# One wait more for a POOL memset, and one filler more, in a decode attention and MLP kernel

## The chip, the cores and the metric

The kernel runs on one core of a Trainium2 chip. The metric is the device time in microseconds (us) of one execution, as the median of several runs. The core has five engines with a queue of instructions each: PE (TensorE, matrix products), DVE (VectorE), ACT (ScalarE), POOL (GpSimd) and SP (which here only issues DMAs). They wait for each other by semaphores.

## The reference

A decode step of one token for 8 sequences: attention over the last 2048 positions of a cache, a small MLP beside it, and a gate that mixes both.

```python
# x: 8 x 1 x 576; caches: 8 x 16 heads x 8192 x 128, bf16; 32 query heads, W = 2048
q = (x @ wq) as 32 heads of 128
k, v = the last W rows of k_cache, v_cache, each head used by two query heads
p = softmax(q k^T * 128**-0.5);  a = (p v) @ wo          # wo: 4096 x 576
y = layernorm(x);  b = gelu(y @ w1 + b1) @ w2 + b2       # w1: 576 x 4608, w2: 4608 x 576
g = sigmoid(sum(x * gate_w));  out = g * a + (1 - g) * b
```

The two caches' windows make up 134 of the 154 MB that are read.

## The kernel before, in words

The keys and values are cut into 16 items each: item n = 4g + i holds 32 of the 128 (sequence, head) pairs (group g) and a quarter i of their window, 4 MB in bf16. Items are loaded in the order K0, K1, V0, K2, V1, ..., K15, V14, V15, each into the next of four slots of the `arena` in SBUF, and then the bias `b2`, the first 24 of 36 column blocks of w2 (two DMAs of 1728 KB), wo (four DMAs of 1152 KB) and the rest of w2 (1152, 432 and 144 KB). All these DMAs are issued by SP in that order (L624, L847, L859, L829); a DMA that reuses a slot makes SP wait until the work that read the slot is done.

For a key item, VectorE transposes four parts (`tr`, L691) and TensorE multiplies each with the queries into four PSUM banks (`qk`, L709 and the helper line L175). VectorE takes the maximum over the banks (`mx`, L642, 128x2048 from PSUM) and updates the running one (`nb`, L646, 128x1), ScalarE takes the exponentials (L648), and VectorE transposes them (`pt`, L666) into `PT`. The result is spread onto the diagonal blocks of a zeroed P tile by four copies, one for each quarter of the partitions (`qrx`, L740 on ScalarE, L741 on POOL or VectorE). Against that tile TensorE multiplies the value item: 64 products, some written out and the others in a loop (`pv`, L753 and the helper line L186). In this text, block n is the 64 products of value item n. VectorE adds the block to the running output (`o`, L796).

For the first 14 items two quarters of the copies go to POOL and two to ScalarE; for items 14 and 15 one goes to ScalarE and three to VectorE (`px_engs`).

The P tile of items 0 to 14 lies at a fixed place, zeroed once by a memset on POOL (`ptx0`, L604); the copies always write the same diagonal blocks. The P tile of item 15, the last, has a home of its own, in the room of the transposed keys (`KT`), which is free once the last `qk` is done. It is zeroed by a second memset on POOL, `o_kz` (`ktx0`, L724, 128x4096 fp32), whose only dependency is that last `qk` (it is added at the end of `k_unit`). The copies of item 15 wait for it (`px_free`). A line near the change orders the maximum of item 15 behind VectorE's three copies of item 14 in VectorE's queue, without a semaphore.

The order in each queue comes from a planner (`_Plan.schedule`), which takes the ready operation with the earliest start by modelled costs; entries in `deps` become semaphore waits, entries in `after` only order.

`keep_warm` issues fillers on TensorE: products of a zero tile with a mask, into a PSUM bank that is not in use. There are ten behind the last `qk` (before block 14), six between blocks 14 and 15, and three (`warm1`) behind the projection with the fourth wo block.

After block 15 come: the sum over the pairs of a group (`vmul`, `acc` on VectorE, `ew` on POOL L804, `us` on TensorE L807), with products of `b2` and w2 beside it on TensorE (`m2_b`, `m2_0`); the output's scaling and transposition (L810, L811); then on TensorE the second 24 products of w2, the four projections with wo (16 products each), `warm1`, and the last 24 products of w2 in three parts (16, 6 and 2), each of which waits for its own DMA. These products have line L580. At last two copies out of PSUM and two small DMAs of the output.

Of the kernel before, what the change touches and what calls it, by code (L numbers as in the profile page):

```python
# [38 lines left out]
class _Plan:  # L39
# [10 lines left out]
    def add(self, eng, fn, deps=(), name=None, cost=0.1, after=(), prio=0):  # L50
        op = _Op(eng, fn, deps, name, cost, after=after, prio=prio)
        op.idx = len(self.all)
        self.all.append(op)
        return op

    def dma(self, eng, fn, semkey, nbytes, deps=(), name=None, after=(), prio=0):
        op = _Op(eng, fn, deps, name, self.DMA_ISSUE, after=after, is_dma=True, dma_sem=semkey, nbytes=nbytes, prio=prio)
        op.idx = len(self.all)
        self.all.append(op)
        return op  # L60
# [113 lines left out]
def held_matmul(nc, e, out, lhsT, rhs, start=False, stop=True, skip=False, tile_size=(128, 128), tile_position=(0, 0)):  # L174
    return e.add_instruction(mybir.InstMatmult(  # L175
        name=nc.get_next_instruction_name(), engine=mybir.EngineType.PE,
        ins=[e.lower_ap(rhs), e.lower_ap(lhsT)], outs=[e.lower_ap(out)],
        start_tensor_calc=start, stop_tensor_calc=stop, is_transpose=False, bass_skip_group_check=skip,
        tile_size=tile_size, tile_position=tile_position, ldweights=False))
# [13 lines left out]
def build_kernel(nc, A_x, A_k_cache, A_v_cache, A_wq, A_wo, B_x, B_w1, B_b1, B_w2, B_b2, gate_w, out):  # L193
# [28 lines left out]
    with ExitStack() as es:  # L222
# [83 lines left out]
        def view(name, parts=128):  # L306
            o, n, dt = R[name]
            a = arena[0:parts, o // 2: o // 2 + (n * (2 if dt == BF else 4)) // 2]
            if dt == F32:
                a = a.bitcast(F32)  # L310
            return a
# [47 lines left out]
        def slot(s):  # L359
            return RAW[:, s * DE:(s + 1) * DE]  # L360
# [247 lines left out]
        pt_done, px_done, pv_done = {}, {-1: [o_px0]}, {}  # L608
# [6 lines left out]
        def take_slot():  # L615
            n = n_slot[0]
            n_slot[0] += 1
            return (1, 2, 0, 3)[n % ND]
# [105 lines left out]
        o_kz = add("pool", lambda e: e.memset(view("KT").bitcast(F32), 0.0), deps=[], name="ktx0", cost=4.5, prio=3)  # L724

        def v_item(n):
# [16 lines left out]

            if n == NL - 2:
                mx_done[n + 1].after.extend(op for op in px_done[n] if op.eng == "dve")

            def pv_part(a, b):
                def fn(e):
                    mm = None
                    for k in range(a, b):  # L750
                        lhsT = bass.AP(arena, offset=px_at + 128 * k, ap=[[AST, 128], [1, 128]])
                        rhs = bass.AP(arena, offset=aoffs("RAW") + s * DE + 128 * k, ap=[[AST, 128], [SE, 2], [1, 128]])
                        mm = e.matmul(ps[:, ob_, 0:256], lhsT, rhs, start=(k == 0), stop=True, skip_group_check=True)  # L753
                    return mm
                return fn
# [60 lines left out]
        def keep_warm(name, n, after, banks=(0, 1, 2, 3), deps=None):  # L816
            def fn(e):
                mm = None
                for k in range(n):
                    args = (ps[:, banks[k % len(banks)], :], zeros_bf, maskR)  # L820
                    mm = e.matmul(*args, start=True, stop=True, skip_group_check=True) if k == 0 else held_matmul(nc, e, *args, start=True, stop=True, skip=True)
                return mm
            return add("pe", fn, deps=[o_z, o_mR] + (deps or [ex_done[NL - 1]]), name=name, cost=0.22 * n, after=after)

        def wo_all(_):
            def place(s, at, i):
                dst = slot(s)[:, at:at + WO_CH * D]
                h0 = WO_CH * i
                d = dma("sp", lambda e: e.dma_start(dst, A_wo[128 * h0:128 * (h0 + WO_CH), :].rearrange("(p j) c -> p (j c)", j=WOR)),  # L829
                        "o%d" % i, WO_CH * 128 * D * 2, deps=slot_free[s] if at == 0 else [], name="d_wo%d" % i, after=last_dma[-1:])  # L830
                last_dma.append(d)
                dj = dst.rearrange("p (j c) -> p j c", j=WOR)
                return AccGroup("proj%d" % i, [(oT[:, j, i, :], dj[:, j, :]) for j in range(WOR)], o_T + [d], cost=1.0, prio=1).op
            s = take_slot()
            done = [place(s, WO_CH * D * i, i) for i in range(3)]
            slot_free[s] = done
            s = take_slot()
            done = [place(s, 0, 3)]
            o_m2.append(keep_warm("warm1", 3, done))
            m2_at.append((s, WO_CH * D))  # L840
            slot_free[s] = done

        m2_at = []
        o_m2 = []
# [36 lines left out]
        for kind, i in stream:  # L881
            {"K": k_item, "V": v_item, "W": wo_all, "M": m2_chunk, "B": bias}[kind](i)
# [64 lines left out]
```

## Time and profile before

| | |
|---|---|
| median of 3 runs | 367.36 us (365.57 to 367.49) |
| the profiled execution | 366.66 us |
| its span | 365.4 us |
| mean granted clock of TensorE | 0.939 |
| busy: PE, DVE, ACT, POOL | 276.6, 256.7, 131.6, 76.1 us |
| data moved | 154.45 MB, 423 GB/s over the span |

All durations and times of day in this document are from the span's start of one profiled execution. The profile names an instruction by engine, line of the kernel, operation, what it writes and reads, and its shape; behind it, in brackets, the idle time of the engine before it and what ended that. Engines that are off the chain of waits may be idle at no cost. The granted clock is the share of TensorE's full speed that it was allowed to run at.

### The profile page before, as it was taken

How to read it: one execution, taken by the hardware profiler on the slowest of the kernel's cores; microseconds unless marked ns; L12 is line 12 of the kernel's file. 1: busy time of each engine (PE TensorE's matmuls, PEld its weight loads, DVE VectorE, ACT ScalarE, POOL GpSimd, SP SyncE). 2: the span in 40 equal slices, each digit the busy share in tenths (PEclk: the TensorE clock that was granted, in tenths of full speed). 3: DMA queues.
4: the chain of work that ended last, by engine and by line, in shares of the span. 5: the costliest groups of instructions: out<-in, count | busy, mean ns of one | idle time of the engine just before them, and what ended most of it. 6: DMA issues, size and time to landing. Idle time of an engine off the chain costs nothing.

```text
span 365.4 us, 4420 instructions
## 1 busy us (share of the span) xinstructions
PE 276.6 (76%) x1829; PEld 126.8 (35%) x1382; DVE 256.7 (70%) x196; ACT 131.6 (36%) x117; POOL 76.1 (21%) x76
## 2 busy tenths in 40 slices
PE   0455555999897958996969669786869697986997
PEld 0110000436171705370525225342516061602774
DVE  0722978797877696949395978767576969499511
ACT  1012106374444442644343325444444444402400
POOL 9123002130414040404121130304040404003000
PEclk9976596999998998999899999999999899999899
DMA  8999999999999999999999999999999999999993
GB/s 347 431 434 407 452 416 446 434 427 448 413 456 407 452 413 452 418 445 434 425 445 416 448 416 445 420 447 416 448 438 423 441 420 442 422 441 416 422 431 155
DMA packets 6578, 154.45 MB, mean 423 GB/s; under 512 B 764, under 2 KB 932, under 8 KB 1320
## 3 DMA queue, kind: packets, MB, share of 16 engines
q1 hardware_dynamic: 6512, 154.29, 98.2%
q8 instruction: 6, 0.10, 0.1%
q10 hardware_dynamic: 56, 0.03, 0.0%
q14 instruction: 4, 0.03, 0.0%
HBM read 154.31 MB, written 0.01 MB: 422 GB/s over the span
## 4 chain that ended last, share of the span: by engine, by line
DMA 45%; DVE 35%; PE 13%; issue 4%; ACT 2%; POOL 0%; ACTq 0%
DMA arena<-in_A_k_cache_dram 43%; DVE arena L691 20%; DVE arena L666 5%; PE ps L175 4%; PE ps L186 4%; DMA arena<-in_gate_w_dram 2%; PE ps L580 2%; DVE arena L642 2%; DVE arena L799 1%; DVE arena L741 1%; PE ps L502 1%; DVE arena L796 1%; PE ps L753 1%; PE ps L709 1%; DVE arena L563 1%
## 5 line engine op out<-in xcount | busy, mean ns | idle before, releaser
L691 DVE STREAM_TRANSPOSE arena<-arena 128x2048 f32<-128x2048 f32 x64 | 144.9, 2287 | 29.9 <-DMA arena<-in_A_k_cache_dram 28.3
L175 PE MATMUL ps<-arena 128*128 128x512 bf16 (+2 forms) x457 | 127.4, 427 | 11.7 <-DVE arena L691 8.7
L186 PE MATMUL ps<-arena 128*128 x942 | 107.1, 275 | 0.0
L186 PEld LDWEIGHTS ps<-arena 128*128 x942 | 92.8, 99 | 11.9 <-issue 0.3
L741 POOL COPY arena<-arena 32x2048 bf16<-32x2048 bf16 x28 | 52.8, 1885 | 206.7 <-DVE arena L666 205.9
L709 PE MATMUL ps<-arena 128*128 128x512 bf16 x120 | 49.3, 411 | 52.6 <-DVE arena L691 45.9
L740 ACT ACTIVATE arena<-arena 32x2048 bf16<-32x2048 bf16 x30 | 57.2, 1906 | 71.9 <-DVE arena L666 71.6
L648 ACT ACTIVATE arena<-ps,arena 128x2048 bf16<-128x2048 f32 x16 | 31.5, 1968 | 108.4 <-DVE arena L646 75.5
L709 PEld LDWEIGHTS ps<-arena 128*128 128x128 bf16 x128 | 13.1, 102 | 163.7 <-DVE arena L691 107.4
L642 DVE TENSOR_REDUCE arena<-ps 128x1 f32<-128x2048 f32 x16 | 36.7, 2291 | 31.8 <-PE ps L175 31.7
L666 DVE STREAM_TRANSPOSE arena<-arena 128x2048 bf16<-128x2048 bf16 x16 | 36.4, 2274 | 2.1 <-ACT arena L648 2.1
L652 ACT ACTIVATE ps<-arena 128x2048 f32<-128x2048 f32 x15 | 28.1, 1872 | 0.1
L753 PE MATMUL ps<-arena 128*128 128x256 bf16 x82 | 14.3, 272 | 3.5 <-DVE arena L741 3.5
L753 PEld LDWEIGHTS ps<-arena 128*128 128x128 bf16 x82 | 8.0, 99 | 18.6 <-issue 16.1
L453 PE MATMUL ps<-arena 8*128 8x8 bf16 x8 | 0.6, 171 | 14.6 <-DVE arena L427 9.5
L558 DVE TENSOR_TENSOR arena<-arena 128x1152 f32<-128x1152 f32 x1 | 1.4, 1358 | 11.5 <-ACT arena L556 11.5
L580 PE MATMUL ps<-arena 128*8 128x288 bf16 (+1 forms) x140 | 9.2, 286 | 0.0
L635 POOL COPY arena<-arena 32x128 bf16<-32x128 bf16 x16 | 4.6, 287 | 15.3 <-ACT arena L537 7.7
L724 POOL MEMSET arena<- 128x4096 f32 x1 | 3.5, 3511 | 20.0 <-PE ps L175 20.0
L804 POOL TENSOR_TENSOR arena<-arena 128x256 f32<-128x256 f32 x4 | 2.5, 613 | 23.7 <-DVE arena L802 23.7
L580 PEld LDWEIGHTS ps<-arena 128*8 128x8 bf16 (+1 forms) x140 | 6.0, 86 | 3.4 <-issue 1.4
L741 DVE COPY arena<-arena 32x2048 bf16<-32x2048 bf16 x6 | 7.0, 1160 | 0.2
(104 smaller groups left out, 94.1 us busy)
## 6 DMA issues: line engine op xcount, KB each, us to landing
arena<-in_A_k_cache_dram SPq DMA_DIRECT2D x16, 4096.0 KB, 27.1
arena<-in_A_v_cache_dram SPq DMA_DIRECT2D x16, 4096.0 KB, 27.0
arena<-in_B_w_dram SPq DMA_DIRECT2D x1, 4608.0 KB, 23.2
arena<-in_A_wo_dram SPq DMA_DIRECT2D x4, 1152.0 KB, 22.5
arena<-in_A_wq_dram SPq DMA_DIRECT2D x1, 4096.0 KB, 12.8
arena<-in_B_w_dram SPq DMA_DIRECT2D x2, 1728.0 KB, 24.5
arena<-in_B_w_dram SPq DMA_DIRECT2D x1, 1152.0 KB, 15.3
arena<-in_B_w_dram SPq DMA_DIRECT2D x1, 576.0 KB, 24.2
```

Source lines behind the costliest of these rows:

```text
L175: return e.add_instruction(mybir.InstMatmult(name=nc.get_next_instruction_name(), engine=mybir.EngineType.PE, ins=[e.lower_ap(rhs), e.lowe ...
L186: return e.add_instruction(mybir.InstMatmult(name=nc.get_next_instruction_name(), engine=mybir.EngineType.PE, ins=[operand(r, r_ap), opera ...
L580: ins = e.matmul(ps[32 * j:32 * j + 8, BK_ACC, 0:JN], lhsT, rhs[:, JN * j:JN * j + JN], start=False, stop=True, skip_group_check=True, til ...
L642: mx = mx_done[n] = add("dve", lambda e: e.tensor_reduce(out=k(n, MX), in_=ps[:, 0:4, :].rearrange("p a n -> p (a n)"), axis=AXL.X, op=ALU ...
L648: ex = add("act", lambda e: e.activation(out=Pm, in_=ps[:, 0:4, :].rearrange("p a n -> p (a n)"), func=ACTF.Exp, bias=k(n, NB), scale=SCAL ...
L652: mask_done[n + 1] = add("act", lambda e: e.activation(out=ps[:, 0:4, :].rearrange("p a (n c) -> p (a n) c", c=32), in_=bass.AP(arena_f, o ...
L666: pt_done[n] = add("dve", lambda e: e.transpose(bass.AP(arena, offset=aoffs("PT") + 2048 * (n % 2), ap=[[AST, 128], [1, 2048]]), Pm), deps ...
L691: tr = add("dve", (lambda rh=rh, hh=hh, kb=kb: lambda e: e.transpose(bass.AP(arena_f, offset=foffs("KT") + kb * 2048, ap=[[AST // 2, 128], ...
L709: mm = e.matmul(*args, start=False, stop=True, skip_group_check=True) if rc == 0 else held_matmul(nc, e, *args, stop=True, skip=True)
L740: return e.activation(out=dst, in_=src, func=ACTF.Copy)
L741: return e.tensor_copy(dst, src)
L753: mm = e.matmul(ps[:, ob_, 0:256], lhsT, rhs, start=(k == 0), stop=True, skip_group_check=True)
```

## The change

Two lines. The memset of the last P tile's home gets VectorE's copies of item 14 (its three quarters of the last P tile but one) as further dependencies, so that POOL waits for a semaphore of VectorE before it. And `warm1`, behind the projection of the fourth wo block (the fourth output block), has four fillers where it had three.

```diff
@@ -743,6 +743,7 @@
 
             if n == NL - 2:
                 mx_done[n + 1].after.extend(op for op in px_done[n] if op.eng == "dve")
+                o_kz.deps.extend(op for op in px_done[n] if op.eng == "dve")
 
             def pv_part(a, b):
                 def fn(e):
@@ -836,7 +837,7 @@
             slot_free[s] = done
             s = take_slot()
             done = [place(s, 0, 3)]
-            o_m2.append(keep_warm("warm1", 3, done))
+            o_m2.append(keep_warm("warm1", 4, done))
             m2_at.append((s, WO_CH * D))
             slot_free[s] = done
```

The order of instructions in all five queues is otherwise the same in both kernels. In POOL's queue the memset stands last but one, with `ew` of the last group (L804) behind it.

## The prediction

> **What bounds the kernel now.** I read the page's slices first: DMA is at 9 tenths in every slice but the last, at 423 GB/s on average, so up to the last key block the kernel runs at the rate at which its data arrive. The chain of waits (window 315 to 366 us) then shows where the order of work takes over:
>
> ```profile
> 318.48 6.61 DVE arena L691 x3
> ...
> 327.73 2.23 DVE arena L666
> ...
> 329.99 3.53 DVE arena L741
> ...
> 333.55 0.69 DVE arena L741
> ...
> 334.27 0.70 DVE arena L741
> ...
> 335.10 0.38 PE ps L753 x2
> ...
> 335.50 8.39 PE ps L186 x60
> ```
>
> From 318.5 us, where the last key block lands, the end is set by VectorE and then TensorE. To be seen: three equal copies of VectorE (L741, its three quarters of P tile 14) take 3.53, 0.69 and 0.70 us, and value block 14 on TensorE waits for the third. The timeline of the same window says what lies beside the slow one, and what it costs later:
>
> ```profile
> 329.47 3.51 POOL L724 MEMSET arena<- 128x4096 f32 x1 [20.05 <-PE ps L175]
> ...
> 334.99 2.29 DVE L642 TENSOR_REDUCE arena<-ps 128x1 f32<-128x2048 f32 x1
> ...
> 341.94 2.12 DVE L741 COPY arena<-arena 32x2048 bf16<-32x2048 bf16 x3
> ...
> 361.79 1.64 PE L580 MATMUL ps<-arena 128*8 128x288 bf16 x24
> ```
>
> The memset ends at 332.98 and the slow copy at 333.52, that is 0.54 us later, about a copy's own length: it has stood still for as long as POOL wrote. The same three copies for P tile 15, with POOL idle, take 2.12 us. An earlier stretch (timeline, 30 to 38 us) repeats it with POOL's other memset, which ends at 36.17:
>
> ```profile
> 32.66 3.51 POOL L604 MEMSET arena<- 128x4096 f32 x1 [5.24 <-PE ps L175]
> 33.80 1.36 DVE L558 TENSOR_TENSOR arena<-arena 128x1152 f32<-128x1152 f32 x1 [11.47 <-ACT arena L556]
> 35.19 1.59 DVE L559 TENSOR_SCALAR arena<-arena 128x1152 f32<-128x1152 f32 x1
> 36.82 1.36 DVE L560 TENSOR_TENSOR arena<-arena 128x1152 f32<-128x1152 f32 x1
> ```
>
> L559 ends 0.61 us behind the memset, while the two-input L558 takes its 1.36 us with the memset running as L560 does without. Last, the stretches of 1 us with the granted clock, third number from the end:
>
> ```profile
> 336.00:337.00 1.00, 1.00 (x9) 0.76 (x8) 1.00 (x1) 0.00 (x0) 0.00 (x0) 0.71 0.81 343
> 337.00:338.00 1.00, 1.00 (x6) 0.71 (x5) 0.44 (x2) 0.49 (x1) 0.00 (x0) 0.50 1.04 444
> ...
> 339.00:340.00 1.00, 1.00 (x7) 0.72 (x6) 0.40 (x1) 0.97 (x4) 0.00 (x0) 0.58 0.97 415
> ```
>
> TensorE stood idle from 331.56 (end of its ten fillers) to 335.10; soon after, its clock is halved from 336.42 to 339.84. The 60 looped matmuls of block 14 take 8.39 us; the same loop for block 12, at full clock (274.08), takes 6.71.
>
> **The change, step by step.**
>
> *The copies.* Without the memset they run 329.99 to 332.14 (2.12 us by the row of P tile 15). Saved: 2.83 us.
>
> *VectorE behind them.* The maximum L642 moves from 334.99 to 332.16 and now has the memset beside it (POOL starts some 0.1 us after the third copy, 332.25 to 335.76). Neither it nor the small L646 behind it is shown beside a memset. L642 reads PSUM; L796, which reads PSUM and SBUF, took 0.44 us beside a POOL copy at 288.33 as it does elsewhere, so I charge nothing; the upper end is a reduction that stands still until 335.76 (rival C). L646 has two SBUF inputs: like L558 beside a memset it would cost nothing, but L799, also with two, took 1.58 us beside a POOL copy (288.81) and 0.48 alone (353.22). The bounds are 0 and 335.76 - 334.47 = 1.3 us. I take 0, as L558 had a memset beside it and not a copy. A gain is excluded, since both already ran undisturbed.
>
> The Trainium skill ("GPSIMD Engine Reference", section Key points) says that POOL and VectorE contend where VectorE is in a two-port mode or has two SBUF inputs. The slow copy agrees; L558, with two inputs, did not slow down. By that rule L646 takes the 1.3 us, and the time below stays the same.
>
> *P tile 15.* Everything up to its copies moves by 2.83: exponentials 334.7, transpose L666 336.8 to 339.1, copies 339.1 to 341.23. The memset must be done by 339.1; it is at 335.76, so its later start is covered by 3.3 us. Behind the new wait POOL's queue holds only L804, needed at 354: nothing.
>
> *Block 14 on TensorE.* The ten fillers still end at 331.56, the block starts at 332.27: idle 0.7 us instead of 3.5, so no half clock; it lasts the 7.0 us of block 12 and ends at 339.3 instead of 344.1. The six fillers then end near 340.6.
>
> *Block 15* waited for block 14 and its fillers; now it waits for the copies: 341.36 instead of 345.38. This is 4.0 us, more than the copies gave, as the half clock goes too. Its 7.29 us end at 348.65.
>
> *The closing stage.* Everything on engines up to the projection moves by 4.0: L807 at 350.9, the next 24 products of w2 at 351.5, projections from 353.1.
>
> *SP.* The wait that holds the fourth block of wo and the last three pieces of w2 is block 14's end, so these four DMAs are issued 4.8 us earlier. They stand behind three wo blocks in one queue, and DMA is at 0.95 to 1.02 from 344 to 359 us. I take nothing for it: they land when they landed before (DMA issues from 344 to 346 us; the last number is us from issue to landing):
>
> ```profile
> arena<-in_A_wo_dram SPq DMA_DIRECT2D x1, 1152.0 KB, 12.9
> arena<-in_B_w_dram SPq DMA_DIRECT2D x1, 1152.0 KB, 15.3
> arena<-in_B_w_dram SPq DMA_DIRECT2D x1, 432.0 KB, 15.9
> arena<-in_B_w_dram SPq DMA_DIRECT2D x1, 144.0 KB, 15.7
> ```
>
> Their issues were at 344.1, 344.51, 344.97 and 345.45, so they land at 357.0, 359.8, 360.9 and 361.15. So the fourth projection, which could start at 356.0, starts at 357.05 and ends at 358.05; four fillers, 0.21 each by the chain (1.08 for five), end at 358.9; then TensorE waits 0.9 us for w2's piece.
>
> *The fourth filler* costs 0.21 us if that wait is not there; in it, nothing.
>
> *The end.* From 359.85 the last 24 products take their 1.64 us and end at 361.5, with the other two pieces landed in time (if they hold up the last eight: 361.75). Before, they ended at 363.43. **Sum: 1.7 to 1.95 us, taken as 1.9.** The remaining 2 us to the span's end are unchanged. The profiled execution, 366.66 us (span 365.4 and 1.26 around it), becomes 364.75. It lies 0.70 below the median of 367.36 of the runs shown; the same step from that median gives **365.4 us**. About half of the 4.0 us won upstream is lost to the data.
>
> **Rivals.**
>
> A. *The data come earlier too.* Issuing 4.8 us sooner could fill the gaps at 359 to 361, where DMA is busy 0.59 and 0.23. For: that share. Against: the queue was 13 to 15 us deep, so those transfers did not wait for their issue. Wholly unblocked, the last products would start at 357.9 and end at 359.55: gain 3.9 us, 363.5; partly, 364.5.
>
> B. *The clock halves at another place.* TensorE now waits 0.7 us before block 15 (1.9 if L646 is held), 1.0 before the fourth projection and 0.9 before the last products. For: an idle 2.41 us was followed by half clock at 288.6. Against: the same 2.41 us before 269.1 was not, and 1.46 and 1.67 us were never. Half clock in block 15 after a held L646: start 342.5, 1.7 us more, end 351.5, last products from 360.8 to 362.4, gain 1.0, 366.4. In the last products: 1.64 more, gain 0.3, 367.1.
>
> The Trainium skill ("TensorE: Matmul & The Clock Gate", Part 1) says that the clock follows activity in windows of about 3.4 us that run freely. The 3.42 us of half clock agree; by it the two waits at the end would have to fill most of one window, which they do not.
>
> C. *Slower: the memset takes the maximum as its victim.* It stands across L642 instead of the copy. If that waits for 335.76 it ends at 338.05, 0.77 later than before, and the copies of P tile 15 end at 344.85. Block 14 ended at 339.3, its fillers at 340.6: TensorE is idle for 4.3 us, and block 15 loses 1.7 us per 3.4 us of half clock, one or two such stretches. It starts at 344.95, 0.43 earlier, ends 1.3 to 3.0 later, and with the fourth filler the end is 1.5 to 3.2 us later: 368.9 to 370.6. It turns into a loss once L642 is held by more than some 2.1 us (4.0 less 1.7 and 0.2); here it is 3.6. For: the long copy was held in just this way. Against: L796 and L691 ran undisturbed beside POOL's copies.
>
> D. *The memset was not at fault*, and 3.53 us belong to that copy: 367.4 to 367.6. The 0.69 and 0.70 behind it speak against it.
>
> **Numbers.** A measurement of this kernel can tell about 0.5%, here 1.84 us, from no change. The forecast has 0.66; its 1.9 lies just beyond that bound, and I put 0.44 above and 0.22 below. A 0.14, B 0.10, C 0.09 (0.01 of it at its lower end, inside the bound), D 0.01. Faster: 0.44 + 0.14 = 0.58. Same: 0.22 + 0.10 + 0.01 + 0.01 = 0.34. Slower: 0.08. The range reaches to 363.9 (most of A) and 366.9 (the forecast with the spread of 1.9 us among the runs shown, and the first B); left out are C and the rests of A, B and D.
>
> **What would show it.** Right: L724 starts near 332.25; three copies of 0.70; L642 of 2.29 and L646 of 0.16 beside the memset; loop of block 14 near 6.7 us at clock 1.00; block 15 from about 341.4; a wait for data of about 1 us before the fourth projection and again behind the fillers; last products from 359.85. Wrong: a long L642; a half clock behind 340; or landings of the last w2 pieces that move with their issue.

## The result and the profile after

The changed kernel takes 364.67 us (median of 5 runs, 364.53 to 364.98) against 366.40 us for five runs of the kernel before on the same occasion: a ratio of 0.9947, with a 95% interval of 0.9925 to 0.9970. By the medians that is 1.7 us or 0.47% faster, by the ratio, which is not that of the medians, 0.53%; the interval excludes no change, but reaches to both sides of the 0.5% that the prediction set as its bound. The profiled execution took 364.70 us, with a span of 363.4 us. Of all runs below, two lie far out and count in no ratio: 415.0 us (one of six of `after_cut`) and 561.8 us (one of the kernel before).

The timeline of the changed kernel, 327 to 336 us. Behind the change, lines from 746 on carry a number that is one higher than before.

```profile
329.96 2.12 DVE L741 COPY arena<-arena 32x2048 bf16<-32x2048 bf16 x3
332.11 2.29 DVE L642 TENSOR_REDUCE arena<-ps 128x1 f32<-128x2048 f32 x1
332.19 3.51 POOL L724 MEMSET arena<- 128x4096 f32 x1 [22.57 <-DVE arena L741]
332.23 0.38 PE L754 MATMUL ps<-arena 128*128 128x256 bf16 x2 [0.70 <-DVE arena L741]
...
334.44 0.16 DVE L646 SCALAR_TENSOR_TENSOR arena<-arena 128x1 f32<-128x1 f32 x1
```

The three copies take 2.12 us together, as those of P tile 15 do. The memset now runs beside the maximum L642 and the small L646, and neither is longer for it: 2.29 and 0.16 us, as before. Block 14 starts after 0.70 us of idle time.

The closing stage in the timeline, 338 to 363 us:

```profile
341.34 0.38 PE L754 MATMUL ps<-arena 128*128 128x256 bf16 x2 [0.34 <-DVE arena L741]
...
351.72 4.58 PE L580 MATMUL ps<-arena 128*8 128x288 bf16 x72
...
357.01 1.15 PE L580 MATMUL ps<-arena 128*8 128x288 bf16 x16 [0.71 <-DMA arena<-in_A_wo_dram]
358.31 0.81 PE L175 MATMUL ps<-arena 128*128 128x512 bf16 x3 [0.16 <-issue]
...
359.78 1.73 PE L580 MATMUL ps<-arena 128*8 128x288 bf16 x24 [0.66 <-DMA arena<-in_B_w_dram]
```

Two waits for data, which the kernel before did not have, stand in the brackets: 0.71 us before the fourth projection and 0.66 us before the last 24 products. The chain of waits (315 to 364 us) says the same of the end:

```profile
332.62 6.72 PE ps L186 x60
...
339.69 0.23 SPq L830
...
339.96 19.77 DMA arena<-in_B_w_dram
...
359.78 1.75 PE ps L580 x24
```

Behind block 14 it no longer goes over VectorE and block 15, but over a w2 piece that SP issued once block 14 was done. Its 19.77 us are nearly all time in the queue, as the landing times show (DMA issues from 339.5 to 342 us, at 339.6, 339.96, 340.43 and 340.9):

```profile
arena<-in_A_wo_dram SPq DMA_DIRECT2D x1, 1152.0 KB, 17.4
arena<-in_B_w_dram SPq DMA_DIRECT2D x1, 1152.0 KB, 19.8
arena<-in_B_w_dram SPq DMA_DIRECT2D x1, 432.0 KB, 20.4
arena<-in_B_w_dram SPq DMA_DIRECT2D x1, 144.0 KB, 20.2
```

Issued 4.5 us earlier, they land at 357.0, 359.8, 360.8 and 361.1: within 0.1 us of where they landed before.

### The profile page after: what moved, and what is told of

It reads as the page before. It is cut to its first block, busy times and chain, and to the rows that moved or that the text cites. A ratio compares the mean times of both kernels' runs of the same rounds, so it can differ in the third digit from the quotient of the medians.

```text
span 363.4 us, 4421 instructions
## 1 busy us (share of the span) xinstructions
PE 274.3 (75%) x1830; PEld 125.7 (35%) x1382; DVE 253.9 (70%) x196; ACT 131.6 (36%) x117; POOL 76.0 (21%) x76
## 4 chain that ended last, share of the span: by engine, by line
DMA 50%; DVE 33%; PE 9%; issue 4%; ACT 2%; ACTq 0%; POOL 0%; SPq 0%
DMA arena<-in_A_k_cache_dram 43%; DVE arena L691 20%; DMA arena<-in_B_w_dram 5%; DVE arena L666 5%; PE ps L175 4%; DMA arena<-in_gate_w_dram 2%; DVE arena L642 2%; PE ps L186 2%; DVE arena L800 1%; PE ps L502 1%; PE ps L709 1%; DVE arena L797 1%; DVE arena L563 1%; DVE arena L741 1%; ACT arena L648 1%
## 5 line engine op out<-in xcount | busy, mean ns | idle before, releaser
L186 PE MATMUL ps<-arena 128*128 x942 | 105.5, 273 | 0.1
L642 DVE TENSOR_REDUCE arena<-ps 128x1 f32<-128x2048 f32 x16 | 36.7, 2291 | 30.9 <-PE ps L175 30.9
L558 DVE TENSOR_TENSOR arena<-arena 128x1152 f32<-128x1152 f32 x1 | 1.4, 1358 | 11.1 <-ACT arena L556 11.1
```

What stands on the lines that cost most here:

```text
L186: return e.add_instruction(mybir.InstMatmult(name=nc.get_next_instruction_name(), engine=mybir.EngineType.PE, ins=[operand(r, r_ap), opera ...
L642: mx = mx_done[n] = add("dve", lambda e: e.tensor_reduce(out=k(n, MX), in_=ps[:, 0:4, :].rearrange("p a n -> p (a n)"), axis=AXL.X, op=ALU ...
```

## Experiments

Theory: the copies stood still behind the memset, and TensorE's idle time behind them halved its clock; together that cost 4 us upstream (that is, up to block 15), of which the landing of the last data hides about half. Rivals: the fourth filler does the work; the half clock cost nothing; the end is not held by data; the copies are slow for another reason. Times and ratios below are against runs of the kernel before on the same chip (366.54 to 366.58 us in median).

**One part at a time.** `dep_only` is the whole change with this edit; `filler_only` is the kernel before with only the fourth filler.

```diff
# dep_only, against the changed kernel
-            o_m2.append(keep_warm("warm1", 4, done))
+            o_m2.append(keep_warm("warm1", 3, done))
# filler_only, against the kernel before
-            o_m2.append(keep_warm("warm1", 3, done))
+            o_m2.append(keep_warm("warm1", 4, done))
```

> The new wait alone, with three fillers behind the projection as before the change. Theory (the last data set the end, the fourth filler lies in the wait for them): the last w2 piece but two lands at 359.8, the fillers end near 359.0 instead of 359.1, the end stays where the whole change has it, 1.7 to 1.9 us under the kernel before (366.4), so 364.5 to 364.8. Rival (the fourth filler keeps TensorE's clock up): half clock in the last 24 products, up to 1.6 us more than the whole change, 365 to 366.3.

Measured: 364.69 us (364.60 to 365.04, 6 runs), ratio 0.9957 (0.9943 to 0.9970).

> The fourth filler alone, on the kernel before. There TensorE comes to the last products at 361.8, two us behind their data, so the filler is not covered: 0.2 us slower than before, 366.5 to 366.7, with 361.8 becoming 362.0. Rival (the filler brings something of its own): 0.2 us or more faster.

Measured: 366.76 us (366.44 to 367.81, 12 runs), ratio 1.0013 (1.0002 to 1.0023). The new wait is the whole gain. The filler alone raises the median by 0.2 us (by the interval, 0.1 to 0.8 us), and beside the wait it changes it by 0.02 us: it lies in the wait for data, which is 0.88 us long with three fillers and 0.66 with four.

**No fillers there.** `no_warm1`:

```diff
# against the changed kernel
-            o_m2.append(keep_warm("warm1", 4, done))
+            o_m2.extend(done)
```

> The whole change, but with none of the fillers behind the projection. Theory (that stretch is a wait for data): the last products start at 359.8 as with four fillers; if the clock stays up, 364.6 as the whole change. Rival B of the prediction (the clock halves after the waits): TensorE idles some 0.7 us before the fourth projection and 1.6 us before the last products, 2.3 us in 3.5; if that is enough, the 24 products take about 3.4 us instead of 1.75 and the time is up to 366.3. An end between 364.5 and 364.8 says the fillers are not needed.

Measured: 364.71 us in the median of 12 runs. Nine lie at 364.50 to 364.87, three at 365.88, 365.96 and 366.26 (ratio 0.9957, 0.9941 to 0.9972). In the profiled execution, one of the nine, TensorE waits 1.62 us for the w2 piece and starts the last products at 359.80, at full clock. So the fillers are not needed in most runs, but three runs lost 1.2 to 1.6 us, and half clock in the last products would cost up to 1.64. No profile was taken of one of those, so that this was the reason is not shown. The next two kernels make the wait longer.

**The last wait made longer.** `held_idle` has no fillers there and holds all 24 last products until the last w2 piece; `held_filled` holds them too and has 14 fillers.

```diff
# against the changed kernel; d's of the three parts are issued first
-                ops.append(AccGroup("m2_%d_%d" % (ci, n), mms, [o_hT, d], ...
+                held = [x for x, _, _ in ds] if ci else [d]
+                ops.append(AccGroup("m2_%d_%d" % (ci, n), mms, [o_hT] + held, ...
-            o_m2.append(keep_warm("warm1", 4, done))
+            o_m2.extend(done)                                 # held_idle
+            o_m2.append(keep_warm("warm1", 14, done))         # held_filled
```

> The whole change without the fillers behind the projection, and all 24 last products held until the last piece of w2 (361.1) instead of each part for its own. TensorE then idles 0.7 us before the fourth projection and 3 us before the last products. Theory (the waits at the end are a place where the clock can halve, as rival B says, and that is what fillers there are for): in most runs the products take up to 3.4 us instead of 1.7; runs spread from 366.0 (clock up: 361.15 + 1.7) to 367.7, median near 367. Rival (half clock does not come there): 366.0, all runs within 0.3 us.

> The same hold until the last piece of w2, with 14 fillers (3.0 us) behind the projection, so that TensorE is busy from 358.3 to 361.4. Theory: clock up in all runs, last products from 361.5, 366.1 to 366.3 with little spread, and so below the median of the kernel with the idle wait. Rival (fillers do nothing for the clock): the same spread as without them.

Measured: 367.31 us (366.07 to 367.60, 12 runs) idle and 366.27 us (366.00 to 367.19, 12 runs) filled. The stretches of `held_idle` (the clock is the third number from the end):

```profile
360.00:361.00 1.00, 0.00 (x0) 0.00 (x0) 0.00 (x0) 0.00 (x0) 0.00 (x0) 0.50 0.27 99
...
362.00:363.00 1.00, 1.00 (x12) 0.57 (x10) 0.00 (x0) 0.00 (x0) 0.00 (x0) 0.50 0.00 0
```

and of `held_filled`:

```profile
360.00:361.00 1.00, 1.00 (x7) 0.00 (x0) 0.00 (x0) 0.00 (x0) 0.00 (x0) 1.00 0.22 81
...
362.00:363.00 1.00, 0.94 (x16) 0.48 (x12) 0.02 (x1) 0.02 (x1) 0.00 (x0) 1.00 0.00 0
```

The same 24 products take 3.05 us in the first, behind 3.14 us of idle time, and 1.64 in the second. The spans of `held_filled` all lie between 364.7 and 365.0 us, so the spread of its times arose outside the span; those of `held_idle` lie between 364.8 and 366.3. Rival B of the prediction is a real cost at this place; in the five runs of the changed kernel, with its shorter waits, it did not come, and 14 fillers prevented it behind the longer one. That three fillers are too few for that and four enough was not shown: none of the 6 runs with three and none of the 5 with four was long.

**The half clock taken away without the new wait.** `fill26`:

```diff
# against the kernel before
-                after.append(keep_warm("warm_pv%d" % n, (10, 6)[n - NL], after, (ob_,), [o_u, o_done[n - 2]]))
+                after.append(keep_warm("warm_pv%d" % n, (26, 6)[n - NL], after, (ob_,), [o_u, o_done[n - 2]]))
```

> The kernel before with 26 fillers instead of ten before block 14, so that TensorE does not idle while the copies of P tile 14 stand still; the copies themselves are as before (3.53, 0.69, 0.70). Theory (of the 4.0 us won upstream 2.8 are the copies and 1.2 the half clock of block 14): fillers end near 334.9, block 14 runs 335.1 to 342.1 at full clock, block 15 then waits for the copies of P tile 15 and starts at 344.2 instead of 345.4, the end is 1.2 us earlier: 365.2. Rival (the half clock cost nothing, block 15 waited for the copies anyway): no change, 366.4.

Measured: 365.71 us (365.46 to 365.89, 12 runs), ratio 0.9978 (0.9967 to 0.9989). From its timeline:

```profile
329.50 5.56 PE L175 MATMUL ps<-arena 128*128 128x512 bf16 x24
...
330.03 4.97 DVE L741 COPY arena<-arena 32x2048 bf16<-32x2048 bf16 x3
...
335.55 6.72 PE L186 MATMUL ps<-arena 128*128 x60
...
344.25 0.38 PE L753 MATMUL ps<-arena 128*128 128x256 bf16 x2 [0.32 <-DVE arena L741]
...
360.84 1.64 PE L580 MATMUL ps<-arena 128*8 128x288 bf16 x24
```

The copies are as slow as before, block 14's loop is back at 6.72 us, and block 15 waits for the copies of P tile 15. The last products start 0.95 us earlier than in the kernel before. The spread shrinks too: 29 runs of the kernel before lie between 365.46 and 367.70, these 12 within 0.43 us. So it is mainly the half clock that scatters: in three profiled executions with an unfilled wait and the copies as before, block 14's loop took 8.39 us (before, 366.66 us in all), 7.82 (`filler_only`, 366.44) and 9.29 (`before_cut` below, 367.50).

**Less data at the end.** `after_cut` and `before_cut` load an eighth of the fourth wo block, in the changed kernel and in the one before.

```diff
-                d = dma("sp", lambda e: e.dma_start(dst, A_wo[...].rearrange("(p j) c -> p (j c)", j=WOR)),
+                cc = D if i == 3 else WO_CH * D
+                d = dma("sp", lambda e: e.dma_start(dst[:, 0:cc], A_wo[...].rearrange("(p j) c -> p (j c)", j=WOR)[:, 0:cc]),
```

> The whole change, with seven eighths of the fourth wo block not loaded (144 KB instead of 1152; its products read what lies in the slot). All later data land 2.4 us earlier (1.03 MB at 427 GB/s): the three w2 pieces near 357.4, 358.4 and 358.7. Theory (behind the change the data set the end, and hide about half of what was won upstream): TensorE now comes to the last products at 358.5 without waiting, and the time falls by a further 1.3 us to 363.3 or 363.4. Rival (something else holds the end, or the 4.0 us upstream are not real): 364.7, as the whole change.

> The kernel before with the same seven eighths of the fourth wo block not loaded. Theory (before the change TensorE's chain sets the end and its data lie waiting two us): no change, 366.4 to 366.6, last products still at 361.8. Rival (the data set the end before too): up to 2.4 us less, 364.1.

Measured: 363.01 us for the changed kernel (6 runs, five of them at 362.85 to 363.11; ratio 0.9894, 0.9873 to 0.9914) and 366.50 for the one before (365.92 to 369.09, 12 runs; ratio 1.0000, 0.9983 to 1.0018). The timeline of `after_cut`:

```profile
351.71 5.56 PE L580 MATMUL ps<-arena 128*8 128x288 bf16 x88
357.43 0.81 PE L175 MATMUL ps<-arena 128*128 128x512 bf16 x3 [0.16 <-issue]
358.17 1.64 PE L580 MATMUL ps<-arena 128*8 128x288 bf16 x24
```

With the data out of the way the projections run without a gap, and the last products start 3.62 us earlier than in the kernel before instead of 2.01. Before the change the same cut is worth nothing. So the data set the end behind the change, not before it, and hid 1.6 us. The expectation for `after_cut` was 0.3 us too late. It had the last products at 358.5 us, near where the changed kernel's fillers end less its wait (359.12 - 0.71); but the fourth projection takes 1.15 us behind a wait and 0.98 without one (5.56 less 4.58), which is 0.17 us of it. The rest is open.

**What holds the copy.** `split_memset` cuts the memset in two; `two_inputs` writes VectorE's copies of P tiles 14 and 15 as a two-input instruction. Both are edits of the kernel before.

```diff
# split_memset
-        o_kz = add("pool", lambda e: e.memset(view("KT").bitcast(F32), 0.0), ...
+            e.memset(view("KT").bitcast(F32)[:, 0:2048], 0.0)
+            return e.memset(view("KT").bitcast(F32)[:, 2048:4096], 0.0)
# two_inputs
+                    if n >= NL - 2:
+                        return e.tensor_tensor(out=dst, in0=src, in1=src, op=ALU.max)
                     return e.tensor_copy(dst, src)
```

> The kernel before with the second memset cut into two of half the size, back to back on POOL from 329.5. Theory (a copy stands still until the POOL instruction that it meets is over): the first copy ends some 0.54 us behind the first half (1.76 us long), near 331.8, instead of 333.5; then either the second half starts at once and holds the next copy until about 333.6 (three copies done near 334.3), or it is itself kept waiting by the copies (done near 333.2). Rival (the copy is slow for the whole time that the tile is being zeroed, whatever the instructions): first copy 3.5 us, as before.

Measured: 366.20 us in a single run; what counts is its trace. From its POOL timeline and its chain:

```profile
329.56 1.80 POOL L725 MEMSET arena<- 128x2048 f32 x1 [20.05 <-PE ps L175]
331.30 2.35 POOL L726 MEMSET arena<- 128x2048 f32 x1
```

```profile
330.08 1.82 DVE arena L744
...
331.93 2.26 DVE arena L744
...
334.22 0.70 DVE arena L744
```

The first copy ends 0.54 us behind the first half (331.36). The second half takes 0.55 us longer than the first, about that copy's length, and the second copy ends 0.54 us behind it (333.65). These times fit two sides that wait for each other's whole instruction, in turn. Both of the outcomes that were expected happened at once, so the three copies end at 334.92, hardly earlier than in the kernel before (334.97); the forecast of 333.2 to 334.3 was too early.

> The kernel before with VectorE's six copies of P tiles 14 and 15 written as a maximum of the source with itself: the same values, but an instruction with two SBUF inputs in place of a copy. Those of P tile 15 have POOL idle and give the length alone (1.1 to 2.2 us each). Theory (a memset holds only copies that take both of VectorE's ways into SBUF, as L559, and not a two-input instruction, as L558): those of P tile 14 beside the memset are as long as those of P tile 15. Rival (what has two SBUF inputs is held too, as L799 beside a POOL copy): the first takes until the memset's end at 333.0 and its own length.

Measured: 365.98 us in a single run. From its timeline:

```profile
329.46 3.51 POOL L724 MEMSET arena<- 128x4096 f32 x1 [19.98 <-PE ps L175]
...
329.98 3.71 DVE L742 TENSOR_TENSOR arena<-arena 32x2048 bf16<-32x2048 bf16 x3
...
340.69 3.71 DVE L742 TENSOR_TENSOR arena<-arena 32x2048 bf16<-32x2048 bf16 x3
```

Beside the memset and without it: 3.71 us for three. A slower instruction form, 1.22 us against 0.70 for a copy, takes 1.25 us less for the three here than copies of which the first stands still (4.96). Its two inputs are one and the same tensor, as those of L558 are; with two different ones only the small L646 (128x1, 0.16 us) ran beside a memset, so for larger instructions of that kind it is not shown.

## Why the prediction was right, point by point

- *The copies*: forecast 2.12 us and an end at 332.14; 2.12 and 332.09.
- *The maximum and L646 beside the memset*: forecast at no cost, with an upper end of 3.6 and 1.3 us; measured 2.29 and 0.16, as before, so rival C falls. The reading that L558 with a memset beside it was the nearer row, and not L799 beside a POOL copy, held, and `two_inputs` shows it on the copies themselves. The Trainium skill ("GPSIMD Engine Reference", section Key points) names two SBUF inputs as a case of contention. With a memset on POOL's side the runs here do not show it (1.22 us for each instruction of `two_inputs`, whose inputs are one tensor, beside the memset as without); beside a POOL copy L799 agrees (1.58 us against 0.48).
- *Block 14 at full clock*: loop forecast at block 12's 6.71, measured 6.72, granted clock 1.00 throughout 327 to 362 us. The whole block was mis-sized, though: the forecast gave it "the 7.0 us of block 12" and an end at 339.3, and it ended at 339.56. Block 12 takes 7.15 us by its own rows (273.86 to 281.01), and a start behind a wait takes 0.17 more (0.39 instead of 0.22 to the loop). So SP's issues came 4.5 us earlier and not 4.8, and the wait before block 15 was 0.34 us and not 0.7; neither reached the end.
- *Block 15*: forecast from 341.36, measured 341.34. Its length was mis-sized: 7.29 us was that of a block that begins right behind fillers. Begun after a wait, its first two products and the start of the loop take 0.43 us instead of 0.21, and it ends 0.2 us later than forecast. This lay in the wait for data.
- *The split of the 4.0 us upstream*: of the 3.82 us by which block 15's loop moved, `fill26` gives the half clock 0.95 in that execution, against 1.2 forecast; the missing part is the same 0.2 us of starting up. The other 2.87 are the copies.
- *SP's earlier issue brings nothing*: landings moved by 0.1 us. Rival A falls.
- *The end*: forecast for the last products 359.85 to 361.5, measured 359.78 to 361.53. The two waits for data were forecast at 1.0 and 0.9 us and measured 0.71 and 0.66, as TensorE came later to them. `after_cut` shows that 1.6 of 3.6 us went to the data, about half, as forecast.
- *The step that failed* is the last: the sum on the profiled execution gave 364.75, and 364.70 was measured; adding 0.70 us to come to the median of the three runs shown gave 365.4. That median was high by chance: with more runs the kernel before has 366.4 to 366.6. Its runs scatter over 2.2 us and the changed kernel's do not, so the difference of one pair of executions should not be carried over to the other. It was luck, too, that the profiled execution before, with 8.39 us in its loop, lay near that later median: the loops of other executions with the same wait took 7.82 and 9.29.
- *The chance of over 0.5%*: 1.9 against 1.84 us was called just beyond the bound, and the ratio's 0.53% with an interval on both sides of the bound is that; the 1.73 us between the medians lie below it.

## What to carry to other kernels

A long instruction of a neighbour that nobody waits for can still stretch the critical path if the two cannot run beside each other, as this memset and these copies: compare the same instruction with and without it before blaming data or dependencies, and move the one that has slack. Count what an idle gap costs behind it too, here a halved clock, and end the sum at the next limit, here a saturated DMA queue whose landing times do not move. Where half of a gain disappears, cutting that limit in both kernels shows it in two runs.

## What the runs showed of the hardware that was not expected

- This memset and these copies alternated by whole instructions: with the memset cut in two, the second half was held by 0.55 us for one copy, and the next copy for all of that half. Shorter memsets alone gave nothing (334.92 against 334.97 us).
- Half clock does not follow a given idle gap at a fixed delay. For the same gap of 3.5 us the loop behind it took 7.82, 8.39 and 9.29 us in three executions; in `filler_only` half clock ran from 334.54 to 337.94, before the block and into it, and in the kernel before from 336.42 to 339.84 (both from the mean clock of stretches of 1 us). In `before_cut` it ran for twice as long, from 333.97 to 340.78. In `two_inputs` a gap of only 2.29 us before block 14 was followed by half clock too, and its loop took 8.14 us. The Trainium skill ("TensorE: Matmul & The Clock Gate", Part 1) has windows of about 3.4 us that are not tied to the kernel's start; the lengths of 3.40, 3.42 and 6.81 us, one window or two, agree.
- That makes the kernel before the noisier one: 29 runs over 2.2 us, against 0.45 us for the changed kernel's five.
